# One 1 MB load of wo in each layer, asked for as a half and three uneven pieces (34, 80 and 14 rows)

## The chip, the core and the metric

The kernel runs on one core of a Trainium2 chip. The metric is the time of one execution on the device in microseconds (us); before the change it is 851.67 us, the median of three runs (850.38 to 851.95). Profiles come from one further execution. The engines are named as the profile names them: PE (matmul) with PEld (its weight loads), DVE (vector), ACT (scalar), POOL, and SP, which here only asks for transfers. The transfers themselves are done by sixteen DMA engines.

## The reference, cut to what matters

Two layers, each an attention block over a cache and a dense block, for 8 batches with one new position each (decode), all in float32. Both layers use the same weights and the same cache:

```python
def _A_ref(x, k_cache, v_cache, wq, wo):      # x: 8 x 1 x 1024, caches: 8 x 4 x 4096 x 128
    q = (x @ wq).reshape(B, Sq, 32, 128).transpose(0, 2, 1, 3)
    k, v = repeat(k_cache, 8, axis=1), repeat(v_cache, 8, axis=1)
    p = softmax(einsum("bhqd,bhkd->bhqk", q, k) * 128 ** -0.5)
    return einsum("bhqk,bhkd->bhqd", p, v).transpose(0, 2, 1, 3).reshape(B, Sq, 4096) @ wo

def _B_ref(x, w1, b1, w2, b2):                # w1: 1024 x 3584
    return gelu(x @ w1 + b1) @ w2 + b2

x = x + _A_ref(_layernorm(x), k_cache, v_cache, wq, wo)
x = x + _B_ref(_layernorm(x), w1, b1, w2, b2)
# and both once more
```

## The kernel before, in words

**Data.** Nearly everything is read from HBM once in each layer: the caches k and v (64 MB each, except six blocks of v that stay on the chip from the first layer to the second), wq, wo, w1 and w2 (14 to 16 MB each). All land in one large tile on the chip, `arena`, 128 rows (partitions) by 52 units of 1024 float32 columns (one unit is 512 KB). A load always fills a number of whole or part units over all 128 rows.

**What sets the order.** The list `stream` holds all loads in the order in which they are wanted, each with its place in the arena: wq, then for each batch k and v, then wo ("o0"), w1, w2, then the second layer in the same way with wo as "o1", w1 as "i1" and last pieces of w2 ("late"). `weights` puts the loads of one matrix into the list; its sizes are in units. wo is listed as

```python
weights(("o0",), wo[0], [4, 4, 2, 2, 4, 4, 4, 4, 4], fixed(40, 44, 48, 50, 40, 44, 48, 40, 44))
weights(("o1",), wo[0], [8, 8, 8, 4, 2, 2], fixed(24, 32, 16, 24, 28, 30))
```

so that the load `(("o0",), 2)` is the third of nine in the first layer and `(("o1",), 4)` the fifth of six in the second, both of two units (128 rows x 2048 columns, 1 MB). `pump` (line 231) takes loads from the head of the list as long as their place is free and asks for each from SP with one `dma_start` (line 241). `release` is called whenever a user is done with a place, and pumps again. SP works through its requests strictly in order; each waits until PE (or another engine) has finished with the place and until what was loaded there before has landed. Each request also takes the next of eight completion counters (DMAHW0 to DMAHW7) in turn, and waits until the load eight requests earlier, which used that counter, has landed.

**Who uses wo.** `project` (line 375) walks over the slots of wo. For each 1024 columns of a slot it issues four matmuls at line 381 (32 columns of `oxT` as weights, 256 columns of wo moving), so a load of two units feeds eight of them. Behind it come the layer norm, `expand` (w1, lines 260 to 296, matmuls at 270 and 273) and, in the second layer, the last matmuls at line 424 (`down_row`), which add w2 to the result, and the store at line 803.

Of the kernel before, what the change touches and what calls it, by code (L numbers as in the profile page):

```python
# [14 lines left out]
P = 128  # L15
# [27 lines left out]
W2_PARTS = (((0, 16, 40), (16, 8, 44), (LAST, 4, 46)), ((0, 4, 47), (4, 16, 48), (20, 4, 46), (LAST, 4, 0)),  # L43
            ((LAST, 4, 1), (0, 16, 2), (16, 8, 6)), ((LAST, 4, 0), (0, 16, 8), (16, 8, 12)))
LATE_AT = 0, 1, 14, 15
LATE = ((0, 0, 4), (1, 0, 4), (2, 0, 2), (3, 0, 2), (2, 2, 2), (3, 2, 1), (3, 3, 1))
LATE_ORDER = [(e, c) for e in range(4) for c in range(CB)]
NGR = F // CH
# [58 lines left out]
def decode_layers(ctx: ExitStack, tc: tile.TileContext, x, kc, vc, wq, wo, w1, w2, out):  # L107


    nc = tc.nc  # L110
# [120 lines left out]
    def pump():  # L231
        while stream:
            key, k, src, starts, keys = stream[0]
            if not k:
                slot = Kept(starts)
            else:
                slot = arena.take(k, [i for i in starts if i + k <= arena.limit])
            if slot is None:
                return
            stream.pop(0)  # L240
            nc.sync.dma_start(out=slot.ap[:, 0:src.shape[1]], in_=src)
            slot.cols = src.shape[1]
            slot.keys = keys
            held[key] = slot

    def release(slot):
        if slot.keys:
            held.update(slot.parts())
            return
        slot.free()  # L250
        pump()
# [8 lines left out]
    def expand(name, rs, work=None):  # L260
        n = 0
        for slot in tiles((name,)):
            for c in range(0, slot.cols, CH):
                u, kt = divmod(n, NT)
                lhs = xnT[:, kt * XS:kt * XS + 32]
                if kt == 0:
                    acc = ps_o.tile([P, CH], F32, tag="o", name="acc")
                if u < NGR - 1:
                    j = kt % 4
                    nc.tensor.matmul(acc[32 * j:32 * j + 32, :], lhs, slot.ap[:, c:c + CH], start=(kt < 4), stop=(kt >= NT - 4))  # L270
                else:
                    for j in range(4):
                        nc.tensor.matmul(acc[32 * j:32 * j + 32, 0:P], lhs, slot.ap[:, c + j * P:c + (j + 1) * P],
                                         start=(kt == 0), stop=(kt == NT - 1))
                n += 1
            release(slot)
            if n % NT:
                continue
            if u == 0:
                flush()  # L280
            if u < NGR - 1:
                row = row_s if work or u % 2 else qz[:, P:P + CH]
                nc.scalar.activation(row, acc, AF.Copy, scale=rs)
                if not work:
                    flush()
                pending.append(lambda u=u, row=row: hidden_wide(u, row))
            else:
                if not work:
                    flush()
                row, hid = row_s[:, 0:P], qz[:, P:2 * P]  # L290
                nc.scalar.activation(row, acc[:, 0:P], AF.Copy, scale=rs)
                nc.vector.transpose(hid, row)
                hidden_group(u, lambda pre: nc.vector.tensor_tensor(pre, hid.rearrange("p (t q) -> p t q", t=GT)[:, :, 0:B], bias1(u), ALU.add))
            for f in (work or {}).get(u, ()):
                f()
        assert n == NGR * NT
# [134 lines left out]
    def arrive(key, kts):  # L431
        slot = held[key]
        for e, kt in enumerate(kts):
            w2_at[key[1], kt] = slot.ap[:, e * Q4:(e + 1) * Q4]
        return kts
# [232 lines left out]
    def opened():  # L668
        arena.limit = N_UNIT
        pump()  # L670
# [14 lines left out]
    def weights(name, dram, sizes, starts, c0=0, i0=0, kept=None):  # L685

        at = c0
        for i, k in enumerate(sizes):
            n = min(int(k * SCW), dram.shape[1])
            k = -int(-k // 1)  # L690
            keys = kept(i) if kept else ()
            stream.append(((name, i0 + i), k, dram[:, at:at + n], starts(k, i), keys))
            at += n
# [26 lines left out]
    def fixed(*at):  # L720
        return lambda k, i: (at[i],)
# [34 lines left out]
    weights(("i1",), w1[0], [4] * 6 + [2, 2], fixed(32, 36, 16, 20, 24, 28, 32, 34))  # L756
    for c, e, n in LATE:
        at = (c * NFT + LAST + e) * Q4
        to = LATE_AT[c] * SCW + e * Q4
        stream.append((("late", c, e), 0 if e else 1, w2[0][:, at:at + n * Q4], arena.ap[:, to:to + n * Q4] if e else (LATE_AT[c],), ()))  # L760
    pump()
    rs = layernorm(x_row, rsum)
    queries(rs)
    for layer in range(2):
# [12 lines left out]
        else:  # L777
# [18 lines left out]
            expand("i1", rs, work)  # L796
            for c, e, n in LATE:
                arrive(("late", c, e), range(LAST + e, LAST + e + n))
# [76 lines left out]
```

## Time and profile before

| | before |
|---|---|
| median of three runs | 851.67 us (850.38 to 851.95) |
| the profiled execution | 851.29 us |
| its span, first to last instruction | 849.5 us |
| PE busy | 548.7 us (65%) |
| DVE busy | 191.0 us (22%) |
| ACT busy | 66.6 us (8%) |
| read from HBM | 358.83 MB, 423 GB/s over the span |
| loads of wo of 1 MB | 4, median 20.6 us from request to landing |

The span and the time of the same execution differ by 1.8 us that lie around the instructions. Times inside the profile count from the start of the span. In a view by windows each row gives a stretch, the busy time of each engine in it with the number of instructions, the clock granted to PE, the mean busy share of the sixteen DMA engines and the rate in GB/s. In the chain of waits each row has a start, a duration and what took that time: followed back from the last instruction, it is always what was waited for last. In the timeline, the brackets at the end of a row tell how long the engine had been idle and what ended that.

### The profile page before, as it was taken

What the parts mean: (1) busy time and instruction counts of PE and PEld (TensorE: products, weight loads), DVE (VectorE), ACT (ScalarE), POOL (GpSimd) and SP (SyncE); (2) the same over time, 40 slices, a digit from 0 to 9 for tenths busy, and PEclk for the clock granted to TensorE, in tenths of its full rate; (3) what the DMA queues carried; (4) which work ended last, traced back from release to release, by engine and by line L of the source; (5) the groups of instructions that cost most, each with busy time, mean ns of one, the idle gap of its engine ahead of it and who ended that gap; (6) DMA issues with size and microseconds to landing.
All of it is one profiled execution on the core that took longest, in us unless ns stands there. A gap on an engine that the chain in (4) does not pass through costs nothing.

```text
span 849.5 us, 9538 instructions
## 1 busy us (share of the span) xinstructions
PE 548.7 (65%) x4090; PEld 190.0 (22%) x4090; DVE 191.0 (22%) x674; ACT 66.6 (8%) x136; POOL 2.2 (0%) x13
## 2 busy tenths in 40 slices
PE   0756665665657557666678785586656666665787
PEld 0212121111212121222233232121211112122333
DVE  0012221312123121400120342131313122221022
ACT  0110000000000000000201100000000000000031
POOL 0000000000000000000000000000000000000000
PEclk9976877778777977858789988768887878888779
DMA  9999999999999999999999999999999999999996
GB/s 401 419 428 434 425 435 424 436 424 436 423 429 437 424 433 423 429 426 424 425 401 413 428 430 423 435 430 433 428 434 430 431 432 429 433 429 432 419 427 280
DMA packets 19770, 359.57 MB, mean 423 GB/s; under 512 B 2192, under 2 KB 2832, under 8 KB 4240
## 3 DMA queue, kind: packets, MB, share of 16 engines
q1 hardware_dynamic: 19584, 358.82, 99.1%
q8 instruction: 32, 0.52, 0.2%
q10 hardware_dynamic: 144, 0.15, 0.1%
q14 instruction: 10, 0.08, 0.0%
HBM read 358.83 MB, written 0.13 MB: 423 GB/s over the span
## 4 chain that ended last, share of the span: by engine, by line
DMA 72%; PE 23%; DVE 2%; issue 1%; another core or an unknown queue 1%; ACT 0%; SPq 0%; DVEq 0%; ACTq 0%
DMA arena<-in_k_dram 29%; DMA arena<-in_v_dram 19%; DMA arena<-in_w_dram 12%; PE sps L545 8%; DMA arena<-in_wo_dram 8%; PE o_ps L600 7%; DMA arena<-in_wq_dram 5%; PE y L381 2%; PE acc L317 1%; PE acc L270 1%; PE sps L577 1%; PE sps L418 1%; PE sps L612 0%; PE sps L590 0%
## 5 line engine op out<-in xcount | busy, mean ns | idle before, releaser
L545 PE MATMUL sps<-arena,qz 128*32 128x512 f32 x1024 | 158.6, 762 | 114.5 <-DMA arena<-in_k_dram 112.5
L600 PE MATMUL o_ps<-arena 128*32 128x512 f32 x512 | 81.3, 765 | 29.2 <-DMA arena<-in_v_dram 29.2
L600 PE MATMUL o_ps<-arena,spare 128*32 128x512 f32 x512 | 83.2, 768 | 24.0 <-DMA arena<-in_v_dram 23.5
L545 PEld LDWEIGHTS sps<-arena,qz 128*32 128x32 f32 x1024 | 35.5, 130 | 202.2 <-issue 116.4
L605 DVE SCALAR_TENSOR_TENSOR scr<-o_ps,bits,scr 128x128 f32<-128x128 f32 x192 | 67.4, 351 | 6.8
L381 PE MATMUL y<-arena,oxT 128*32 128x256 f32 x512 | 46.7, 532 | 27.8 <-DMA arena<-in_wo_dram 27.7
L603 DVE TENSOR_SCALAR scr<-o_ps,bits 128x128 f32<-128x128 f32 x64 | 22.5, 351 | 145.6 <-PE o_ps L600 145.6
L270 PE MATMUL acc<-arena,oxT 128*32 128x512 f32 x192 | 31.5, 787 | 10.8 <-DMA arena<-in_w_dram 10.5
L612 PEld LDWEIGHTS sps<-bits,scr 128*128 128x128 f32 x128 | 22.1, 217 | 67.8 <-issue 45.1
L317 PE MATMUL acc<-arena,oxT 128*32 128x512 f32 x248 | 32.7, 669 | 5.4 <-DMA arena<-in_wq_dram 3.9
L568 ACT ACTIVATE arena<-arena,bits 128x512 f32<-128x512 f32 x16 | 11.4, 714 | 271.5 <-DVE scr L563 271.5
L613 DVE TENSOR_TENSOR oxT<-sps,scr 128x8 f32<-128x8 f32 x64 | 10.6, 165 | 94.7 <-PE sps L612 94.7
L381 PEld LDWEIGHTS y<-arena,oxT 128*32 128x32 f32 x512 | 20.1, 147 | 51.7 <-DMA arena<-in_wo_dram 26.2
L568 ACT ACTIVATE spare<-spare,bits 128x512 f32<-128x512 f32 x16 | 11.4, 714 | 257.1 <-DVE scr L563 257.1
L600 PEld LDWEIGHTS o_ps<-arena 128*32 128x32 f32 x512 | 16.6, 128 | 61.0 <-issue 46.6
L550 DVE TENSOR_SCALAR_CACHE_REDUCE arena<-sps 128x512 f32<-128x512 f32 x16 | 11.1, 692 | 82.2 <-PE sps L545 82.2
L550 DVE TENSOR_SCALAR_CACHE_REDUCE spare<-sps 128x512 f32<-128x512 f32 x16 | 11.1, 692 | 81.7 <-PE sps L545 81.7
L600 PEld LDWEIGHTS o_ps<-arena,spare 128*32 128x32 f32 x512 | 16.7, 128 | 54.1 <-issue 46.3
L612 PE MATMUL sps<-bits,scr 128*128 128x8 f32 x128 | 28.0, 291 | 0.0
L559 PE MATMUL sps<-scr,bits 128*128 128x128 f32 x32 | 8.0, 333 | 24.2 <-DVE scr L555 24.2
L577 PE MATMUL sps<-ident,arena 128*128 128x128 f32 x64 | 14.9, 399 | 12.6 <-ACT arena L568 12.5
L577 PE MATMUL sps<-ident,spare 128*128 128x128 f32 x64 | 11.9, 324 | 12.5 <-ACT spare L568 12.2
(131 smaller groups left out, 280.6 us busy)
## 6 DMA issues: line engine op xcount, KB each, us to landing
arena<-in_v_dram SPq DMA_DIRECT2D x26, 4096.0 KB, 21.6
arena<-in_k_dram SPq DMA_DIRECT2D x21, 4096.0 KB, 21.0
arena<-in_k_dram SPq DMA_DIRECT2D x20, 2048.0 KB, 17.6
arena<-in_w_dram SPq DMA_DIRECT2D x17, 2048.0 KB, 12.7
arena<-in_v_dram SPq DMA_DIRECT2D x9, 2048.0 KB, 18.2
arena<-in_wo_dram SPq DMA_DIRECT2D x8, 2048.0 KB, 12.4
arena<-in_wo_dram SPq DMA_DIRECT2D x3, 4096.0 KB, 23.6
arena<-in_w_dram SPq DMA_DIRECT2D x5, 1024.0 KB, 12.4
```

The lines of the kernel that those rows point to most:

```text
L270: nc.tensor.matmul(acc[32 * j:32 * j + 32, :], lhs, slot.ap[:, c:c + CH], start=(kt < 4), stop=(kt >= NT - 4))
L317: nc.tensor.matmul(acc[u][32 * j:32 * j + 32, d0 - j * CH:d1 - j * CH], xnT[:, kt * XS:kt * XS + 32], ap[:, d0 - c0:d1 - c0], start=(kt == ...
L381: nc.tensor.matmul(y[32 * j:32 * j + 32, 0:Q4], lhs[:, n * B:n * B + 32], slot.ap[:, c + j * Q4:c + (j + 1) * Q4], start=(n == 0), stop=(n ...
L545: nc.tensor.matmul(ps[32 * g:32 * g + 32, :], qz[:, c:c + 32], kt[:, g * CH:(g + 1) * CH], start=(j == 0), stop=(j == HKV - 1))
L550: nc.vector.tensor_scalar(st["row", b].ap[:, half * CH:(half + 1) * CH], ps, SCALE, None, op0=ALU.mult, op1=ALU.max, accum_out=st["mx", b] ...
L568: nc.scalar.activation(part, part, AF.Exp, bias=bias, scale=1.0, accum_out=ls[:, h:h + 1])
L577: nc.tensor.transpose(pp[:, t * P:(t + 1) * P], row[:, c:c + P], ident)
L600: nc.tensor.matmul(o[32 * g:32 * g + 32, :], s[:, g], v[:, g * CH:(g + 1) * CH], start=(half == 0), stop=(half == NH - 1))
L603: nc.vector.tensor_scalar(r, o[:, 0:P], sel_t[:, 0:1], None, op0=ALU.mult)
L605: nc.vector.scalar_tensor_tensor(r, o[:, t * P:(t + 1) * P], sel_t[:, t:t + 1], r, op0=ALU.mult, op1=ALU.add)
L612: nc.tensor.matmul(po[:, 0:REP], r_s[j % 2], sel_h, start=True, stop=True)
L613: nc.vector.tensor_tensor(oT_v[:, j * REP:(j + 1) * REP, b], po[:, 0:REP], rl_s[b % 2][:, j * REP:(j + 1) * REP], ALU.mult)
```

## The change

The load named in `UNEVEN` is asked for in four requests where it was one. The first brings columns 0 to 1023 of all 128 rows, the other three bring columns 1024 to 2047, for rows 0 to 33, 34 to 113 and 114 to 127. All other loads stay whole. The names in the list are tuples such as `("o0",)`, and the table writes them so.

```diff
+UNEVEN = (("o0",), 2), (("o1",), 4)
+ROWS = (0, 34), (34, 114), (114, P)
...
-            nc.sync.dma_start(out=slot.ap[:, 0:src.shape[1]], in_=src)
+            n = src.shape[1]
+            half = n // 2 if key in UNEVEN else n
+            nc.sync.dma_start(out=slot.ap[:, 0:half], in_=src[:, 0:half])
+            if half < n:
+                for p0, p1 in ROWS:
+                    nc.sync.dma_start(out=slot.ap[p0:p1, half:n], in_=src[p0:p1, half:n])
```

On SP, in the first layer, the requests for wo stood like this before (DMAHW is a completion counter of an earlier load, the other names in brackets are engines waited for):

```order
L241 DMA arena<-in_wo_dram 128x4096 [waits DMAHW3_49,PE_49]
L241 DMA arena<-in_wo_dram 128x4096 [waits DMAHW4_49,PE_49]
L241 DMA arena<-in_wo_dram 128x2048
L241 DMA arena<-in_wo_dram 128x2048 [waits DVE_49,PE_49,Activation_49]
L241 DMA arena<-in_wo_dram 128x4096 [waits DMAHW7_49,PE_49]
L241 DMA arena<-in_wo_dram 128x4096 [waits DMAHW0_49,PE_49]
```

and with the change:

```order
L245 DMA arena<-in_wo_dram 128x4096 [waits DMAHW3_49,PE_49]
L245 DMA arena<-in_wo_dram 128x4096 [waits DMAHW4_49,PE_49]
L245 DMA arena<-in_wo_dram 128x1024
L248 DMA arena<-in_wo_dram 34x1024
L248 DMA arena<-in_wo_dram 80x1024
L248 DMA arena<-in_wo_dram 14x1024
L245 DMA arena<-in_wo_dram 128x2048 [waits DVE_49,DMAHW5_49,PE_49,Activation_49]
L245 DMA arena<-in_wo_dram 128x4096 [waits DMAHW7_49,DMAHW6_49,PE_49]
L245 DMA arena<-in_wo_dram 128x4096 [waits DMAHW0_49,PE_49]
```

The third request has become four, none of which waits for anything new. The request behind them now also waits for counter 5, that is for the load eight requests earlier, which is the 4 MB load among the last batch's three of v; in the profile of before PE starts on it at 352.18 us.

On PE, in `project`, the third and fourth load of wo were used like this before:

```order
L381 MATMUL y<-arena,oxT 32x256 [waits DMAHW1_49]
L381 MATMUL y<-arena,oxT 32x256 x7
L381 MATMUL y<-arena,oxT 32x256 [waits DMAHW2_49]
L381 MATMUL y<-arena,oxT 32x256 x7
L381 MATMUL y<-arena,oxT 32x256 [waits DMAHW3_49]
```

and with the change:

```order
L388 MATMUL y<-arena,oxT 32x256 [waits DMAHW1_49]
L388 MATMUL y<-arena,oxT 32x256 x3
L388 MATMUL y<-arena,oxT 32x256 [waits DMAHW4_49,DMAHW3_49,DMAHW2_49]
L388 MATMUL y<-arena,oxT 32x256 x3
L388 MATMUL y<-arena,oxT 32x256 [waits DMAHW5_49]
```

The first four matmuls of the load wait for its first half alone, the other four for all three pieces. The number and order of the matmuls are the same.

## The prediction

> **What bounds the kernel now.** I read the page first, for which engine carries the end.
>
> ```profile
> span 849.5 us, 9538 instructions
> ...
> q1 hardware_dynamic: 19584, 358.82, 99.1%
> q8 instruction: 32, 0.52, 0.2%
> ...
> q14 instruction: 10, 0.08, 0.0%
> ...
> DMA 72%; PE 23%; DVE 2%; issue 1%; another core or an unknown queue 1%; ACT 0%; SPq 0%; DVEq 0%; ACTq 0%
> ```
>
> Queue 1 (all loads that SP asks for) keeps the sixteen DMA engines busy for 99.1% of the span, and transfers are 72% of the chain that ended last. So the kernel ends when the DMA engines have moved 358.82 MB, and the only thing left to win or lose there is how evenly the sixteen finish. The packet count tells how a load is shared: SP issues 135 loads and one store, 19,584 / 136 = 144 = 128 rows + 16, so each load of 128 rows leaves 8 rows and one closing packet on each of sixteen engines. All sixteen thus have the same rows to move; what differs is the rest, 32 instruction packets of PE (0.52 MB) on queue 8 and 10 on queue 14, of which each falls on one engine.
>
> Next the windows at the very end, where the share of busy DMA engines times 16 is a count of engines still at work.
>
> ```profile
> core 0: us, PE busy (x) PEld busy (x) DVE busy (x) ACT busy (x) POOL busy (x), PEclk, DMA share, GB/s
> 840.00:840.50 0.50, 0.04 (x4) 0.04 (x6) 0.21 (x2) 0.06 (x1) 0.00 (x0) 1.00 1.01 383
> ...
> 842.50:843.00 0.50, 0.50 (x16) 0.20 (x8) 0.43 (x3) 0.00 (x0) 0.00 (x0) 1.00 0.58 213
> ...
> 843.50:844.00 0.50, 0.37 (x6) 0.15 (x6) 0.07 (x1) 0.00 (x0) 0.00 (x0) 1.00 0.26 92
> 844.00:844.50 0.50, 0.47 (x10) 0.16 (x8) 0.00 (x0) 0.00 (x0) 0.00 (x0) 1.00 0.10 35
> 844.50:845.00 0.50, 0.50 (x15) 0.29 (x8) 0.00 (x0) 0.00 (x0) 0.00 (x0) 1.00 0.06 23
> 845.00:845.50 0.50, 0.50 (x12) 0.28 (x10) 0.00 (x0) 0.00 (x0) 0.00 (x0) 1.00 0.02 6
> 845.50:846.00 0.50, 0.50 (x11) 0.24 (x3) 0.00 (x0) 0.00 (x0) 0.00 (x0) 1.00 0.00 0
> ```
>
> All sixteen work until 840.5. At 842.5 to 843.0 it is 0.58 x 16 = 9, at 843.5 to 844.0 four, and from 844.5 to 845.2 a single one (0.06 x 16 = 1; 0.02 x 16 x 0.5 us = 0.16 us of one engine after 845.0). The engines are up to 4.7 us apart: seven stop early, nine late, and the last one alone sets the end. That the end follows it is in the chain of waits and in the timeline:
>
> ```profile
> 813.76 26.66 DMA arena<-in_w_dram
> 840.42 0.04 issue
> 840.46 1.12 PE acc L273 x32
> ...
> 844.29 0.80 PEld L424 LDWEIGHTS sps<-arena,oxT 128*32 128x32 f32 x16 [0.51 <-DMA arena<-in_w_dram]
> 845.31 0.57 PEld L424 LDWEIGHTS sps<-arena,oxT 128*32 128x32 f32 x10 [0.22 <-DMA arena<-in_w_dram]
> ```
>
> A load counts as landed when its slowest engine is done, so L273 starts at 840.46 by the late engine, and the last weight loads of L424 still wait for it at 844.29 and 845.31. A microsecond more or less on the last engine is a microsecond of the kernel.
>
> **The change part by part.** The load named in each layer (2048 columns, 8 KB a row) becomes its first half (128 rows of 4 KB) and its second half in 34, 80 and 14 rows of 4 KB. Bytes stay the same. The price of a row comes from the long even stretch; that of short rows from a stretch where rows of 4 KB move:
>
> ```profile
> 500.00:780.00 280.00, 179.10 (x1150) 57.46 (x1154) 74.51 (x251) 14.82 (x35) 0.00 (x0) 0.81 1.00 431
> ...
> 444.00:445.00 1.00, 1.00 (x16) 0.33 (x12) 0.00 (x0) 0.00 (x0) 0.00 (x0) 1.00 0.67 238
> ...
> 446.00:447.00 1.00, 1.00 (x24) 0.57 (x20) 0.00 (x0) 0.00 (x0) 0.00 (x0) 1.00 1.06 397
> 447.00:448.00 1.00, 1.00 (x24) 0.60 (x20) 0.00 (x0) 0.00 (x0) 0.00 (x0) 1.00 1.04 393
> ```
>
> 431 GB/s over sixteen engines is 26.9 GB/s for one, so a row of 4 KB takes 4096 / 26.9 = 0.152 us.
>
> *How the pieces are shared* decides everything, and no load of this trace has other than 128 rows. Below, they stay as even as rows allow: 34 rows as 3 or 2, 80 as 5, 14 as 1 or none, so 7 to 9 rows where 8 were, at most 0.15 us either way for an engine and layer. Above, shares stay equal, as in all 136 transfers counted here: equal whole-row shares on at most sixteen engines are 80 = 16 x 5, 14 = 14 x 1 and 34 = 2 x 17. I take the equal ones, the only way of sharing that the packet count shows. Then, against 8 rows on each engine:
>
> - the pair that gets 34: 17 + 5 + 1 = 23 rows, +15 x 0.152 = +2.28 us
> - twelve engines: 5 + 1 = 6, -2 x 0.152 = -0.30 us
> - two engines without the 14: 5, -3 x 0.152 = -0.46 us
>
> [...]
>
> *Shorter rows.* From 446 to 448, where rows of 4 KB move, the engines bring 395 GB/s with all of them busy, against 431. If all of that is the row length, the load's 8 x 8 KB = 64 KB on one engine take 2.65 instead of 2.43 us, +0.2 us; if none of it is (an instruction packet in that stretch would show the same way), nothing. I take +0.1, half way. Per layer then: pair +2.4, twelve -0.2, two -0.36; for both layers +4.8, -0.4, -0.7.
>
> *Three more requests on SP.* Each takes 0.33 us of SP, 1.0 us a layer, and the eight completion counters come round sooner: a load waits until the load eight before it has landed.
>
> ```profile
> 348.94 0.81 SPq L241 DMA_DIRECT2D arena<-in_wo_dram  x2
> 359.18 0.33 SPq L241 DMA_DIRECT2D arena<-in_wo_dram  x1
> ...
> 340.00:372.00 32.00, 21.99 (x172) 9.15 (x164) 9.01 (x31) 2.12 (x5) 0.00 (x0) 0.78 1.00 426
> ...
> 352.18 1.92 PE L600 MATMUL o_ps<-arena 128*32 128x512 f32 x16 [2.97 <-DMA arena<-in_v_dram]
> ...
> 366.88 6.22 PE L381 MATMUL y<-arena,oxT 128*32 128x256 f32 x64 [0.65 <-DMA arena<-in_wo_dram]
> 376.92 3.64 PE L381 MATMUL y<-arena,oxT 128*32 128x256 f32 x32 [3.82 <-DMA arena<-in_wo_dram]
> ```
>
> The 1 MB load behind the pieces went out at about 349.4; now it waits for the 4 MB of v that PE starts on at 352.18, some 2.8 us later. Behind it on SP stands only the request of 359.18, so nobody is held up. PE reads the pieces inside the run that begins at 366.88, 14 us later, and the engines are full meanwhile (share 1.00 from 340 to 372). Cost nothing under this cover; without it 2.8 us.
>
> *PE* waits at L381 once more inside the load: four matmuls can begin on the first half, the next four need three counters. The first half comes no later than the whole did, so this costs nothing of its own; how late the pair's 17 rows are is counted above.
>
> **The sum.** If the later of the pair is one of the nine late engines (they stop between 842.8 and 845.2), it stops 4.8 us later, at 847.6 to 850.0, which is 2.4 to 4.8 us after today's last. Middle: +3.6 us. The profiled execution took 851.29 us (0.4 under the median of the runs, 851.67), so 851.29 + 3.6 = **854.9 us**, with 853.7 to 856.1 as its own range.
>
> **Rivals.** (1) *The pair is early, not slower.* If both engines stop before 842.6, they can take 2.4 us in the second layer and still end with the others. The end then follows an engine with fewer rows: -0.4 to -0.7 us, 850.6 to 850.9. For it: seven of sixteen stop early. Against: both must be among them, 7/16 x 6/15 = 0.18 if engines are unrelated, 7/16 = 0.44 if the two are always alike. It decides at one point: whether a pair engine still moves after 842.6. [...]
>
> (2) *Half of it is lost.* Between the layers some engines do run dry (share 0.67 from 444 to 445, five of sixteen idle). If the pair is late and yet has its first 2.4 us swallowed there, only the second layer's stays: 0 to +2.4, middle 852.5. Against: who runs dry is who is ahead, and the pair would be behind.
>
> (3) *The shares stay even*, so the change does not do what the odd numbers of rows say: within 0.3 us for both layers plus 0.2 for short rows, 851.0 to 851.8.
>
> **How the numbers follow.** The forecast has 0.44, rival 1 has 0.34 (between its bounds, leaning to the upper), rival 2 0.14, rival 3 0.08. 0.2% is 1.7 us, about what a measurement of this kernel can tell from no change (its runs lie from 850.38 to 851.95). The forecast is all slower, of rival 2 not quite half: 0.50. Faster by that much needs rival 1 and luck in the runs, since evening out all sixteen could win only the idle share after 840.5: 0.06. Same: 0.44. The range has to take in rival 1 and the forecast: 850.4 to 856.1.
>
> **What would show it.** In the changed profile's last windows: a stretch of 2 to 4 us with a share near 0.06 to 0.12 (one or two engines) after the others have stopped, and idle before L424 for DMA grown by as much; PE's wait for wo at L381 longer than 0.65 and 3.82 us in the first layer. If instead the share falls as before and ends by 845, the pair was early; if it is unchanged to a tenth, the shares are even. Wrong altogether would be a gain over 2 us, or a loss that shows before 340 us, where nothing is changed.

## The result, and the profile after

The change made the kernel slower by 0.63%: the ratio to the kernel before is 1.0063 (95% interval 1.0046 to 1.008), 857.17 us against 851.94 us as medians of six runs each, so 5.2 us more.

| | before | change |
|---|---|---|
| median of six runs | 851.94 us (850.38 to 852.67) | 857.17 us (855.53 to 859.0) |
| profiled execution | 851.29 us | 855.53 us |
| its span | 849.5 us | 853.8 us |
| PE, DVE, ACT busy | 548.7, 191.0, 66.6 us | 540.2, 191.0, 66.6 us |

The profiled execution of the change is the fastest of its six, so its span shows 4.3 of the 5.2 us. No engine has more to compute. From the page of the change, the packets of queue 1:

```profile
span 853.8 us, 9551 instructions
...
q1 hardware_dynamic: 19904, 358.82, 99.3%
```

The bytes are those of before, the packets 320 more, 160 for each layer. A whole load leaves 128 + 16 = 144. With the first half whole (144), 34 rows on 2 engines (36 with the closing packets), 80 on 16 (96) and 14 on 14 (28) a layer has 304, which is 160 more; with all pieces on sixteen engines it would be 176 more. The total alone could be split otherwise, but the run that loads the 34 rows aside (below) has 180 more packets a layer, 144 + 34 + 2, and what then remains for 80 and 14 rows is the most that they can have. The packets under 512 B say the same: 2192 before, 2256 with the change and 2228 in that run, so 32 and 18 more a layer, as 2 + 16 + 14 and 16 + 2 closing packets give. So, at one closing packet an engine, the pieces go to the 2, 16 and 14 engines that the prediction took. That each engine gets an equal share (17, 5 and 1 rows) fits the count and stays the author's estimate.

Where the time goes is seen in the windows over the split load, here of the kernel before (busy time of each engine, PE clock, DMA share, GB/s):

```profile
364.00:372.00 8.00, 7.23 (x66) 3.12 (x58) 0.17 (x1) 0.00 (x0) 0.00 (x0) 0.54 1.03 428
...
798.00:808.00 10.00, 7.49 (x108) 3.48 (x100) 0.43 (x2) 0.00 (x0) 0.00 (x0) 0.84 1.02 428
```

and of the change:

```profile
364.00:372.00 8.00, 3.92 (x42) 1.92 (x42) 0.17 (x1) 0.00 (x0) 0.00 (x0) 0.73 1.02 268
...
500.00:780.00 280.00, 178.89 (x1142) 59.65 (x1138) 75.00 (x252) 14.81 (x35) 0.00 (x0) 0.82 1.00 431
...
798.00:808.00 10.00, 7.23 (x97) 3.26 (x88) 0.00 (x0) 0.00 (x0) 0.00 (x0) 0.84 1.02 289
```

All sixteen DMA engines are busy in both kernels (share 1.02 to 1.03), but with the change they move 268 GB/s for 8 us in the first layer and 289 GB/s for 10 us in the second, instead of 428. Lost are 8 x (428 - 268) / 428 = 3.0 us in the first layer and 10 x (428 - 289) / 428 = 3.2 us in the second; between them the rate is the 431 GB/s of before. A busy share near 1 thus says nothing of speed here: the GB/s beside it must be read too. PE waits for it in the timeline of the change:

```profile
362.21 1.93 PE L388 MATMUL y<-arena,oxT 128*32 128x256 f32 x32 [0.89 <-DMA arena<-in_wo_dram]
...
368.55 5.35 PE L388 MATMUL y<-arena,oxT 128*32 128x256 f32 x48 [4.08 <-DMA arena<-in_wo_dram]
374.64 1.07 PE L388 MATMUL y<-arena,oxT 128*32 128x256 f32 x16 [0.75 <-DMA arena<-in_wo_dram]
379.55 3.64 PE L388 MATMUL y<-arena,oxT 128*32 128x256 f32 x32 [3.83 <-DMA arena<-in_wo_dram]
```

The wait that was 0.65 us before the second run of matmuls is now 4.08 us; the one that was 3.82 us is 3.83 us. And the windows at the end of the change:

```profile
845.00:845.50 0.50, 0.50 (x28) 0.50 (x24) 0.37 (x2) 0.23 (x1) 0.00 (x0) 1.00 1.02 389
845.50:846.00 0.50, 0.50 (x24) 0.41 (x16) 0.01 (x1) 0.01 (x1) 0.00 (x0) 1.00 0.88 332
...
847.50:848.00 0.50, 0.14 (x7) 0.05 (x6) 0.30 (x2) 0.15 (x1) 0.00 (x0) 1.00 0.83 285
848.00:848.50 0.50, 0.50 (x6) 0.10 (x6) 0.00 (x0) 0.00 (x0) 0.00 (x0) 1.00 0.53 186
848.50:849.00 0.50, 0.50 (x11) 0.28 (x11) 0.00 (x0) 0.00 (x0) 0.00 (x0) 1.00 0.23 78
849.00:849.50 0.50, 0.50 (x13) 0.26 (x5) 0.00 (x0) 0.00 (x0) 0.00 (x0) 1.00 0.09 31
849.50:850.00 0.50, 0.50 (x13) 0.27 (x9) 0.00 (x0) 0.00 (x0) 0.00 (x0) 1.00 0.00 0
```

There is no long stretch with one or two engines left, as two very late engines would give. The shares fall from 845.5 to 849.5 in 4.0 us, where they took 4.7 us before: the sixteen end a little closer together than they did. The end is late because all of them are late.

### The profile page after: what moved, and what is told of

It reads as the page before. It is cut to its first block, busy times and chain, and to the rows that moved or that the text cites. A ratio compares the mean times of both kernels' runs of the same rounds, so it can differ in the third digit from the quotient of the medians.

```text
span 853.8 us, 9551 instructions
## 1 busy us (share of the span) xinstructions
PE 540.2 (63%) x4090; PEld 188.8 (22%) x4090; DVE 191.0 (22%) x674; ACT 66.6 (8%) x136; POOL 2.2 (0%) x13
## 2 busy tenths in 40 slices
DMA packets 20090, 359.57 MB, mean 421 GB/s; under 512 B 2256, under 2 KB 2896, under 8 KB 4816
## 3 DMA queue, kind: packets, MB, share of 16 engines
q1 hardware_dynamic: 19904, 358.82, 99.3%
## 4 chain that ended last, share of the span: by engine, by line
DMA 70%; PE 25%; DVE 2%; issue 1%; another core or an unknown queue 1%; ACT 0%; SPq 0%; DVEq 0%; ACTq 0%
DMA arena<-in_k_dram 31%; DMA arena<-in_v_dram 14%; DMA arena<-in_wo_dram 12%; DMA arena<-in_w_dram 9%; PE sps L552 9%; PE o_ps L607 7%; DMA arena<-in_wq_dram 5%; PE y L388 2%; PE acc L324 1%; PE sps L584 1%; PE sps L425 1%; PE acc L277 1%; PE sps L431 1%; DVE spare L557 0%
## 5 line engine op out<-in xcount | busy, mean ns | idle before, releaser
L607 PE MATMUL o_ps<-arena,spare 128*32 128x512 f32 x512 | 78.7, 730 | 16.5 <-DMA arena<-in_v_dram 15.7
L388 PE MATMUL y<-arena,oxT 128*32 128x256 f32 x512 | 43.9, 502 | 35.3 <-DMA arena<-in_wo_dram 35.3
L277 PE MATMUL acc<-arena,oxT 128*32 128x512 f32 x192 | 28.9, 729 | 13.5 <-DMA arena<-in_w_dram 13.5
L619 PEld LDWEIGHTS sps<-bits,scr 128*128 128x128 f32 x128 | 21.7, 213 | 66.6 <-issue 42.3
L324 PE MATMUL acc<-arena,oxT 128*32 128x512 f32 x248 | 32.3, 662 | 5.8 <-DMA arena<-in_wq_dram 4.3
L584 PE MATMUL sps<-ident,spare 128*128 128x128 f32 x64 | 14.2, 383 | 12.3 <-ACT spare L575 12.2
```

The costliest lines, as they stand in the source:

```text
L324: nc.tensor.matmul(acc[u][32 * j:32 * j + 32, d0 - j * CH:d1 - j * CH], xnT[:, kt * XS:kt * XS + 32], ap[:, d0 - c0:d1 - c0], start=(kt == ...
L388: nc.tensor.matmul(y[32 * j:32 * j + 32, 0:Q4], lhs[:, n * B:n * B + 32], slot.ap[:, c + j * Q4:c + (j + 1) * Q4], start=(n == 0), stop=(n ...
L584: nc.tensor.transpose(pp[:, t * P:(t + 1) * P], row[:, c:c + P], ident)
L607: nc.tensor.matmul(o[32 * g:32 * g + 32, :], s[:, g], v[:, g * CH:(g + 1) * CH], start=(half == 0), stop=(half == NH - 1))
L619: nc.tensor.matmul(po[:, 0:REP], r_s[j % 2], sel_h, start=True, stop=True)
```

## The experiments

The theory after this reading, called **crossing** and a supposition until the runs speak: a piece with fewer than 128 rows puts its rows on other engines than a whole load does, and there they collide at their destination on the chip with rows of the loads around them. Its rivals: the **pair** with 17 rows holds up the rest (the forecast), or **short rows** and more requests cost the time. Each kernel was timed in five rounds beside the kernel before on the same chip; its ratio is to those runs. All edits are to `pump` or its table, against the change.

**Halves: no piece of rows.**

```diff
-ROWS = (0, 34), (34, 114), (114, P)
+ROWS = ((0, P),)
```

> Each of the two loads in two requests, both halves for all 128 rows: no piece of rows is left. Crossing theory (a piece that is not 128 rows puts its rows on other engines than a whole load does, and these collide at their destination): as before, 851.9 us within 1 us, and the windows over wo stay above 400 GB/s. Pair theory (the two engines with 17 rows hold up the rest): also as before. Short-row theory (rows of 4 KB and more requests are the cost): the same row length as the change in all of the load, so at least half of the change's 5.2 us stays, 854.5 us or more.

Measured: 851.02 us, ratio 1.0002 (0.9992 to 1.0013). Windows:

```profile
364.00:372.00 8.00, 4.51 (x74) 2.18 (x66) 0.31 (x3) 0.00 (x0) 0.00 (x0) 1.00 1.02 418
```

Rows of 4 KB and one more request cost nothing that shows, at 418 GB/s. The short-row theory falls.

**Even row pieces.**

```diff
-ROWS = (0, 34), (34, 114), (114, P)
+ROWS = (0, 64), (64, P)
```

> The second half in rows 0 to 63 and 64 to 127: four rows on every engine in each piece, so all sixteen engines have the same share as in a whole load. Crossing theory: windows over the load well under 400 GB/s and 853.5 to 857 us. Pair theory: no pair is left, 851.9 us within 1 us. Short-row theory: like the halves with one request more.

Measured: 857.22 us, ratio 1.0071 (1.0057 to 1.0084).

```profile
364.00:372.00 8.00, 4.13 (x46) 2.12 (x42) 0.17 (x1) 0.00 (x0) 0.00 (x0) 0.79 1.03 268
```

The loss is all there, at the change's own 268 GB/s, and each piece is on sixteen engines by the packet count (19904, so 160 more a layer: 2 x (64 + 16)), four rows each if they share equally. Neither uneven shares nor odd counts are needed for it.

**The change without its pair.**

```diff
-ROWS = (0, 34), (34, 114), (114, P)
+ROWS = (0, 32), (32, 34), (34, 114), (114, P)
```

> The change with its 34 rows as 32 and 2: the two engines have 2 + 1 + 5 + 1 = 9 rows where the change gives them 23. Pair theory: nearly all of the loss goes, 852.5 us or less. Crossing theory: rows still come by other engines than in a whole load, 854 to 857 us, with windows over the load still under 400 GB/s.

Measured: 858.19 us, ratio 1.0077 (1.0063 to 1.0091).

```profile
364.00:372.00 8.00, 4.11 (x42) 1.83 (x42) 0.17 (x1) 0.00 (x0) 0.00 (x0) 0.79 1.03 266
```

Taking 14 of 23 rows from the pair wins nothing.

**The pair without the crossing.** Both halves whole, and the 34 rows once more into HBM:

```diff
-                for p0, p1 in ROWS:
-                    nc.sync.dma_start(out=slot.ap[p0:p1, half:n], in_=src[p0:p1, half:n])
+                nc.sync.dma_start(out=slot.ap[:, half:n], in_=src[:, half:n])
+                aside = nc.dram_tensor(f"aside_{key[0][0]}", (34, n - half), F32, kind="Internal").ap()
+                nc.sync.dma_start(out=aside, in_=src[0:34, half:n])
```

> Both halves for all 128 rows, and the 34 rows of the second half once more, into a scratch tensor in HBM: the two engines get 17 rows more, without any row taken off its engine on the way into the chip. Pair theory: the pair is as late as in the change, by 2.4 us a layer, 854 to 857 us. Crossing theory: windows over the load stay above 400 GB/s and the time depends on whether the pair was early: 851.9 to 853 us if so, 854.3 to 856.7 us if the pair is among the nine late engines.

Measured: 850.44 us, ratio 0.9997 (0.9988 to 1.0006).

```profile
364.00:372.00 8.00, 4.99 (x54) 2.47 (x50) 0.17 (x1) 0.00 (x0) 0.00 (x0) 0.79 1.01 419
```

Seventeen rows more on each of the two engines, in both layers, cost at most 0.06%, 0.5 us. The pair has room for them. In the packet records a row begins within a few ns of the end of the row before on its engine (of the kernel before, from 500 to 780 us, mostly 3 or 4 ns ahead of the recorded end), so rows can be linked to engines, though not without ambiguity. In the second layer of this run the two chains with the extra rows begin the first half at 795.2 and 796.2 us, as first and seventh of the sixteen (795.2 to 799.2), and go on to the next load at 800.4 and 801.4, before the last of all does so at 801.7. So the pair is among the early engines there, even with the 17 extra rows of the first layer behind it. With the run before, the pair theory falls twice.

**The same pieces, another destination.** Both halves whole, and the second half once more as rows 0 to 63 and 64 to 127, into HBM:

```diff
+                nc.sync.dma_start(out=slot.ap[:, half:n], in_=src[:, half:n])
                 for p0, p1 in ROWS:            # (0, 64), (64, P)
-                    nc.sync.dma_start(out=slot.ap[p0:p1, half:n], in_=src[p0:p1, half:n])
+                    aside = nc.dram_tensor(f"aside_{key[0][0]}_{p0}", (p1 - p0, n - half), F32, kind="Internal").ap()
+                    nc.sync.dma_start(out=aside, in_=src[p0:p1, half:n])
```

> Both halves for all 128 rows, and the second half once more as rows 0 to 63 and 64 to 127, into a scratch tensor in HBM. If rows collide at their destination on the chip: only the extra 0.5 MB counts, 0.5 MB at 431 GB/s = 1.2 us a layer, 852 to 854 us, and no row of 4 KB takes much over the 0.16 us of the halves. If the sixteen engines are slow on such pieces wherever they go (reading from HBM, or making the requests): the 1.2 us and the loss of the row pieces, 858 us or more.

Measured: 853.88 us, ratio 1.0037 (1.0025 to 1.0049), 3.2 us (2.1 to 4.2) where the extra bytes alone are 2.4.

```profile
364.00:372.00 8.00, 7.29 (x66) 3.60 (x70) 0.17 (x1) 0.00 (x0) 0.00 (x0) 0.50 1.01 417
```

The same two pieces from the same source, asked for in the same way, slow nothing down when they go to HBM: 417 GB/s against 268. So what slows them is at the destination on the chip. That it is rows of other loads they meet there is the theory's reading; the runs show the place, not the partner. The single packet records of the traces say the same, here those of the first layer from 345 to 395 us (the last column: what all packets of queue 1 took over the usual time of their size, summed and divided by sixteen):

```
               4 KB packets   mean    up to 170 ns   extra per engine
before                    0      -          -             0.34 us
change                  256   243 ns       66             3.15 us
halves                  256   163 ns      254             0.33 us
even row pieces         256   242 ns       72             3.43 us
without the pair        256   244 ns       75             3.25 us
pair aside, to HBM      290   162 ns      288             0.28 us
64 rows aside, to HBM   384   162 ns      380             0.29 us
```

An undisturbed row of 4 KB takes about 0.16 us; in the change three of four take more than 170 ns. Half of the 4 KB packets there belong to the first half, which has all 128 rows, so whole loads beside the pieces are held up too. The next whole load shows it as well: its 128 rows of 8 KB take 453 ns on average in the change, 314 ns in the halves.

**A quarter of the bytes.** Rows 0 to 63 and 64 to 127 as above, for 256 columns only:

```diff
-            half = n // 2 if key in UNEVEN else n
+            half = n - Q4 if key in UNEVEN else n
```

> Rows 0 to 63 and 64 to 127 for the last 256 columns of the load alone, the first 1792 for all 128 rows: a quarter of the bytes cross, in as many requests. Price by bytes: a quarter of the 6.5 us of the 64-row pieces, 1.6 us, 852.2 us. Price by request or by the time that engines are apart: most of it stays, 855 us or more.

Measured: 852.0 us, ratio 1.0015 (1.0007 to 1.0024), 1.3 us (0.6 to 2.0).

```profile
364.00:372.00 8.00, 4.93 (x66) 2.46 (x62) 0.17 (x1) 0.00 (x0) 0.00 (x0) 0.85 1.02 370
```

As many requests as with the half, a fifth of its loss (1.3 of 6.0 us by the ratios): the price goes with the bytes of the pieces, not with the number of requests.

**Twice the bytes.** Rows 0 to 63 and 64 to 127 for both halves:

```diff
-            nc.sync.dma_start(out=slot.ap[:, 0:half], in_=src[:, 0:half])
+            if half == n:
+                nc.sync.dma_start(out=slot.ap[:, 0:half], in_=src[:, 0:half])
             if half < n:
+                for p0, p1 in ROWS:            # (0, 64), (64, P)
+                    nc.sync.dma_start(out=slot.ap[p0:p1, 0:half], in_=src[p0:p1, 0:half])
                 for p0, p1 in ROWS:
                     nc.sync.dma_start(out=slot.ap[p0:p1, half:n], in_=src[p0:p1, half:n])
```

> Rows 0 to 63 and 64 to 127 for both halves: twice the bytes cross. Price by bytes: twice the 6.5 us, 863.5 us. Price by the time that engines are apart: 858 to 860 us.

Measured: 860.35 us, ratio 1.0114 (1.0101 to 1.0128), 9.7 us.

```profile
364.00:374.00 10.00, 4.73 (x54) 2.33 (x50) 0.17 (x1) 0.00 (x0) 0.00 (x0) 0.76 1.04 235
```

About 1.6 times the loss of the half (9.7 against 6.0 us by the ratios), not twice: between the two expectations. With pieces behind pieces, less of what crosses meets rows of a whole load; that reading is argued, not shown.

**The first layer alone.**

```diff
-UNEVEN = (("o0",), 2), (("o1",), 4)
+UNEVEN = ((("o0",), 2),)
```

> The change in the first layer alone. The loss of a layer stays with it: half of the change's, 853.2 us; if the layer change swallowed the first one, 850.7 us; if only the first counted, 856 us.

Measured: 854.82 us, ratio 1.0042 (1.0028 to 1.0055), 3.6 us (2.4 to 4.7).

```profile
364.00:372.00 8.00, 4.00 (x41) 1.91 (x40) 0.17 (x1) 0.00 (x0) 0.00 (x0) 0.79 1.03 261
798.00:808.00 10.00, 8.60 (x124) 4.02 (x116) 0.00 (x0) 0.00 (x0) 0.00 (x0) 0.82 1.01 424
```

The first layer's loss reaches the end, at least for the most part, and the second layer runs at its old rate. Half of the change's loss, 2.6 us, lies within the interval.

**Which rows are at home.** A row is called at home when the engine that brings it is the one that would bring it in a whole load. Which engine brings which row is shown by no trace here; that one order of the rows keeps more of them at home than another is a supposition of the author's. Two twins, each with four pieces of 8 rows and one of 96, for the second half, differ in the order of the rows alone. The stride:

```diff
-                for p0, p1 in ROWS:
-                    nc.sync.dma_start(out=slot.ap[p0:p1, half:n], in_=src[p0:p1, half:n])
+                for r in range(4):
+                    nc.sync.dma_start(out=slot.ap[r:32:4, half:n], in_=src[r:32:4, half:n])
+                nc.sync.dma_start(out=slot.ap[32:P, half:n], in_=src[32:P, half:n])
```

> Second half as four pieces of 8 rows, every fourth row of rows 0 to 31 (0, 4, ... 28; then 1, 5, ... 29; and so on), and rows 32 to 127. [...] If the order of rows is without meaning: the same as its twin.

and with `slot.ap[8 * r:8 * r + 8, half:n]` in place of the stride:

> [...] If the order of rows is without meaning: the same as the twin.

Measured: the stride 855.66 us, ratio 1.0058 (1.0042 to 1.0075); the block 857.05 us, 1.0065 (1.0051 to 1.0079). The stride is lower by 1.4 us, and the intervals overlap. So once more with all 2048 columns:

```diff
-ROWS = (0, 34), (34, 114), (114, P)
+ROWS = *(slice(r, 32, 4) for r in range(4)), slice(32, P)
...
-            half = n // 2 if key in UNEVEN else n
-            nc.sync.dma_start(out=slot.ap[:, 0:half], in_=src[:, 0:half])
-            if half < n:
-                for p0, p1 in ROWS:
-                    nc.sync.dma_start(out=slot.ap[p0:p1, half:n], in_=src[p0:p1, half:n])
+            for rows in ROWS if key in UNEVEN else (slice(0, P),):
+                nc.sync.dma_start(out=slot.ap[rows, 0:n], in_=src[rows])
```

> The stride of the run before the last (four pieces of every fourth row of rows 0 to 31, then rows 32 to 127), now for all 2048 columns of the load: 0.75 MB crosses if the four pieces stay on their own engines, at the 9.7 us that 1 MB a layer cost 7.3 us, 858 us. If the order of rows is without meaning: the same as its twin, 860 to 861 us.

and its twin with `slice(8 * r, 8 * r + 8)`:

> Its twin with blocks of 8 rows, all 2048 columns: the whole 1 MB crosses, 9.7 us, 860 to 861 us, 2 to 3 us more than the stride. If the order of rows is without meaning: the same as the stride.

Measured: the stride 861.96 us, 1.0114 (1.0094 to 1.0135); the block 863.56 us, 1.0138 (1.0115 to 1.0161). Both are slower than expected, and again the stride is lower by 1.6 us with overlapping intervals. The profiled executions alone would have it the other way in the second pair, with spans of 861.7 and 859.8 us, but in the windows over the loads (364 to 374 and 798 to 808 us) the stride has the higher rate each time: 316 and 312 GB/s against 299 and 301, then 254 and 350 against 220 and 277. A price for the order of the rows fits both pairs, but is not settled; that it comes from rows at home is not shown.

## Why the prediction was wrong

The direction was right, the size was not (857.17 us measured, 854.9 forecast, range to 856.1), and the mechanism behind the size was another one; so the direction came out right by luck.

- **What bounds the kernel** held: lost DMA time makes the kernel longer. By the packet records the change is 1.15 MB behind the kernel before at 400 us, 0.85 MB at 500, 0.90 MB at 780 and 2.12 MB at 840. The last is 4.9 us at 431 GB/s; less the 0.7 us or so by which the sixteen now end closer together, it is 4.2 us, against 4.3 us between the two spans. The 0.30 MB (0.7 us) regained between the layers need not be the change's doing: the halves and the aside run, which lose nothing, regain 0.18 and 0.37 MB there against the same profile.
- **How the pieces are shared** held: the packet count, with 32 closing packets more a layer, shows 2, 16 and 14 engines.
- **The step that failed** is the one that prices a moved row: "a row of 4 KB takes 4096 / 26.9 = 0.152 us", wherever it is put, so that +15 rows are +2.28 us for the pair and -2 rows a gain for the rest. The runs show that row pieces bound for the chip cost time on all sixteen. Half a megabyte a layer, 1.2 us of sixteen engines at the full rate, cost 2.6 us more than that when it came in row pieces (5.2 us over two layers), in even pieces (6.0 us by the ratio, 4.8 to 7.1) as in uneven ones. This term had no place in the sum; the sum had nothing in its stead but the pair. Why the destination slows them stays open: that rows meet those of other loads there is the theory's reading, and the twins did not settle it.
- **The pair** was forecast among the nine late engines. The run that loads its 17 rows aside shows it early and at no loss, so +4.8 us for it did not come. The count of seven early engines out of sixteen gave no ground for which two; a run that gives the pair more to do without touching the rest was the way to know.
- **Shorter rows**, +0.2 us at the upper end and +0.1 taken for each layer: 0.0002 of the time with an interval of 0.001 for both layers, so no more than 1.1 us in all and not told from nothing.
- **Three more requests and the counters** cost nothing under their cover, as forecast: the halves have one more request in each layer and the aside run two, both at the old time (ratios 1.0002 and 0.9997). One row was misread on the way: the request of 349.4 us is the split load itself, and the 1 MB load behind it is the request of 359.18, which is later than 352.18 anyway. So the 2.8 us were no risk, cover or not.
- **Rival 1** (the pair is early, 850.6 to 850.9) had the pair right, but its time did not come either (857.17 us), for the loss is not the pair's. The runs show that the destination on the chip decides (417 GB/s to HBM, 268 to the chip); they do not show what happens there.
- **Rival 2** (half of it lost between the layers) falls with the run of the first layer alone, which keeps 2.4 to 4.7 us. **Rival 3** (even shares) falls with the packet count.

No version tried beats the kernel before: the halves and the aside run are level with it within 0.13%.

## What to carry to other kernels

On a queue that keeps all sixteen DMA engines full, as this one does, split a load by columns, not by rows: here two halves of 128 rows cost nothing that shows (ratio 1.0002), while pieces of rows cut the rate of everything around them from 428 to 268 GB/s for 8 us. Evening out engines by handing rows to the early ones lost time here in every division of rows that was tried (ratios 1.0015 to 1.0138). And before an engine's lateness is priced, test whether it is late: load something for it aside.

## What the runs showed that was not expected

The price of a row in such a piece is more than a fair share of the rate: 1.2 us worth of bytes cost 2.6 to 3.3 us a layer on top, two to three times as much. The two pieces of 64 rows, with sixteen engines on each piece, were no better than 34, 80 and 14 (1.0071 and 1.0063, intervals overlapping).
